# Another listed order for the first 1881 instructions of a fused attention and max-of-three-matmuls kernel

## The chip, the cores and the metric

The kernel runs on one core of one Trainium2 chip. Its time is the device time of one execution in microseconds (us); less is better. The core has five engines that work side by side, each with its own instruction stream that it takes strictly in order: PE (matmuls), DVE (vector work), ACT (activation functions and copies), POOL (elementwise work) and SP, which here only issues DMA transfers. An instruction that waits for another engine holds up everything listed behind it on its own engine.

## The reference

Local and global tokens attend to each other in 8 batches of 8 heads (512 local and 32 global tokens, head size 64). Local tokens see the global ones and a window of 32 to each side; global tokens see all. The heads are then joined and go through an elementwise maximum of three matmuls and a last matmul, all in f32:

```python
s_g = scale * np.matmul(q_g, k_all.transpose(0, 1, 3, 2))
out_g = np.matmul(sm(s_g), v_all)
s_ll = np.where(mask, scale * np.matmul(q_l, k_l.transpose(0, 1, 3, 2)), -1000000000.0)
s_l = np.concatenate([scale * np.matmul(q_l, k_g.transpose(0, 1, 3, 2)), s_ll], axis=-1)
out_l = np.matmul(sm(s_l), np.concatenate([v_g, v_l], axis=2))
x = np.concatenate([out_g, out_l], axis=2).transpose(0, 2, 1, 3).reshape(B * S, H * D)   # 4352 x 512 at S = 544
h = np.maximum(np.maximum(x @ w1, x @ w2), x @ w3)      # 512 -> 768, three times
out = h @ w_out                                          # 768 -> 512
```

## The kernel before

**Attention** goes slot by slot: a slot is 128 local tokens of a pair of heads. For each slot PE computes scores (`S`, or `pm` where they sit in a bank of the later matmuls; L368 from `kn` and `qn`, L372 from `kst` and `qs`); DVE evicts them with mask and row minimum (L375); ACT takes the exponential (L377); DVE sums and inverts (`z`, L379, L380); POOL or ACT scales (L120 to L124; in the first 16 slots the scaled tile is `s`, later `prob`, copied there by a DMA `prob<-s`); PE transposes (L408, `T`); ACT or DVE copies the transposed tile out (`pt`, L109 and L111; from slot 16 on in two steps, a rounded copy on ACT and the remainder by L103 on DVE); PE multiplies with V (L467 or L474, `O`); and `O` is evicted to `xr`. The 32 global tokens of each pair of heads take their own chain: scores at L294 or L298, their minimum at L302 and L310, the exponential on ACT at L311, the sum and its inverse on DVE at L312 and L313 (`zg`), the scaling to `probg`, and a transpose at L433, whose result goes into a bank of `S` and from there into `pt`.

**The matmuls behind it** work in rounded f32 with a remainder: every operand is held as a rounded half and what is missing (`xs` hi and lo, made from `xr` on ACT or DVE and on POOL at L103; weights `wh`/`wl`, `woh`/`wol`). L527 multiplies `xs` with `wh` and `wl` for the three weight matrices, twice hi and once lo; DVE takes the maximum (L535); the result is split into `h` (ACT L111, POOL L103); L546 multiplies with `woh`/`wol`.

**The weights** come in 24 pieces, `m` = 0 to 17 for `wh0` to `wh5` (three each) and six for `woh`. Each piece passes five engines in turn in `convert`: a DMA into `wraw`, ACT L162, POOL L165, DVE L169, L170 and L171 (through one PSUM bank `W` that all pieces share), ACT L174 (the rounded half), POOL L177 (the remainder).

**Order.** The body first issues the instructions in a nominal order; a running list of them is `traced`. Then `in_order` ties each instruction named in the table `FIRST` to the one named before it by a dependency without a semaphore, so that the table's order becomes the order of every engine's own stream; what the table does not name comes behind, in nominal order. `8+2` in the table means 8, 9, 10. Semaphores for data are as before in any order. The table covers the start, all weight pieces, the attention of slots 0 to 33 (two of the eight batches, and the start of the third) and the first matmuls behind it. Of a run of 821.5 us the listed part fills the first 172; behind it each engine's stream has the same order in both kernels.

The table is read at build time only:

```python
turn = [k for a, n in pairs for k in range(int(a), int(a) + int(n) + 1)]
for a, b in zip(turn, turn[1:]):
    tc.add_manual_dep(traced[b], traced[a].name, info, reason="order")
```

Of the kernel before, what the change touches and what calls it, by code (L numbers as in the profile page):

```python
# [687 lines left out]
8 4 0 5+1 9+2 1+1 13 7 3 45 14 138 15 217 26 304 37 39 52 54 40 16 38 17 65 27 41 76 28 42 12 113 18 53 20 19  # L688
29 99 21 31 1233 43 30 44 1281 22+1 46 24 32 47 77+1 25 50 33+1 48 79 35 80 49 55+1 51 36 66 81 67 57 82 59 58
105 167 68 60 84 70 85+2 69 61+1 106 71 63 83 107 64 88 72 89 73 90 108 74 119 134 120 75 135 91 93 100+1 92  # L690
251 102 136 103 121 94 109 157 123 114 137 104 115 95 110 116 96 117 139 122 141 158 97 118 129+1 142 131 98
132 159 124 198 140 152 161 143 111 133 144 153 148 154+1 125 199 145 126 150 160 156 127 173 346 162 128 146
193 200 194 151 195+1 163 168 201 169 164 174 170+1 183 175 202 177 172 165 176 197 213 166 178 203 236+1 208+2
112 211 204+1 238+1 184 206 179 147 212 234 190 180 214 235 181 240 207 182 280+3 187 149 186 188 408 226 409
189 228 185 227 410+2 229 413 264 432 438 230 215 192 265 216 439 218 440+1 220 442 219 452 221 453 222+2 241
272 242 225 191 252+2 243 255 257 245 231 244 454 259 246 266 477+2 256 1084 284 267 232 331 268 332+2 269 258
233 273 247 261 274 313 262 270 260 295+2 248 275 298 285+1 277 300 263 299 276 329 249 301 425 414 287 445 250
480 271 289 330 315 288 290 302 316 426+1 278 446+1 481+1 291 303 314 317+1 307 292 305 308 323 279 306 310+1
336+1 309 324 322 321 312 325 335 347+2 1282 350 338 320 352 356 363 340 293 364+2 319 294 368+1 355 339 494
370 351 353 372 569 341 378+1 326 380 327 381 342+1 383 385 415 357 416 367 354 358 371 403+2 382 406 360 359  # L700
384 373 433+2 344 417 361 436 328 443 387 345 386 390 388 401 393 407 374 428 448 389 483 418 472+1 375 474 419
362 475 394 868 395 484+1 420 402 396 437 444 376 568 429 476 486 430 449 377 450 397 495 487 496 456 504+1 391
421 506 392 422 507 488 515 545 431 546+1 455 457 548 558 451 398 500 497 489 501 423 502 458 503 510 508 511
424 516 512 399 513 459 514 517 464 518+1 543 521 460 522+1 498 524+2 490 549+1 400 509 551 461 552+1 491 465
554+1 557 544 466 559 570 462 571 467 499 572+3 560 576+1 469 520 578 468 579 561 581+1 492 583 556 584 580 463
585 493 528 589 529 591+1 527 593+1 590 595 562 596+2 530 599 470 617+3 1283 586 622 563 623+1 1098 531 626+1
621 628 535 629+1 564 631 587 471 565 641 536 642+1 640 632 644 532 566 645+1 634 852 647+1 533 588 649 537 650
653 633 654 656 538 601 600 657+1 625 659 661 635 662 539 663+2 651 666+1 660 655 567 668 689 534 669 691 636
692 652 540 602 693+1 696 637 697 670 698 541 690 699 603 700+3 695 704 609 604 705+2 639 709+1 605 671 711+2
715 606 542 610 717+2 638 720 714 611 721+1 724 672 725+1 723 612 727+2 673 731 708 732 716 733 751+2 613 754  # L710
756+2 755 759+1 763 730 761 608 762 607 764+1 776 674 614 777 781 775 766 782+1 681 784 768 767 785 675 786+2
615 791 676 793+1 769 734 795+1 678 797 677 798 789 800 824 801+1 804 683 805 799 616 825 806 682 807+2 684 826
679 827+1 735 829 831+1 778 833 830 834 685 835+1 838 779 840+1 770 686 680 736 790 853 771 792 780 854+1 737
851 856+2 743 803 859 738 860+2 876 837 877+1 687 879 739 880 884 772 886+1 863 888 842 773 885 889 688 890 744
891 844 892 740 774 893 864 894 843 912 881 913 810 914 916 745 845 917+3 741 921 746 933 839 865 747 934+1 931
748 936+2 846 882 742 847 939 866 940 867 941 811 848 812 942 945 883 946 849 948 813 895 949+1 953 749 954 817
850 955 922 956+2 915 814 907+1 923 909+1 959+1 924 961 750 818 975 815 947 976+1 911 962 978 869 819 991 925
992+1 896 870 820 943 994 968 1022 871 1023 821 816 1024+1 872 969 963 926 1002 944 1038 897 927 1039 873 822
1040+1 1003 874 964 898 970+3 875 1004 899 902 1049 974 1050+1 900 1068+3 928 903 1085 1007 1054 929 951 823
979 965 980 930 952 1008 932 981 995+2 983 998 901 990 982 1000 984 1009+1 904 1005 999 1055+1 905 1006 1057  # L720
1086 906 1042 1017+2 1001 1020 966 1043+2 985 1087 986 1021 1026 967 1011 1016 987 1012 1027 988 1046+1 989
1058 1028 1013 1030 1059 1029 1037 1060 1048 1052 1094 1014 1072+1 1031 1015 1088 1095 1106 1032 1107 1033 1083
1108 1074 1111 1113 1034 1076 1114 1053 1115 1061 1116 1096 1035 1097 1089 1112 1075 1063 1099 1064 1036 1065+1
1090+1 1077 1092 1062 1109 1117 1067 1118 1078 1125 1110 1100 1126+1 1093 1079 1128+2 1101 1080 1141 1081 1102
1142 1144 1131 1145+1 1133 1147 1103 1132 1148 1143 1120+2 1134 1104 1123 1149 1152 1124 1153 1135 1154 1105
1136 1157+1 1150 1159 1137 1160+1 1151 1082 1162+1 1138 1172+1 1155 1164 1174 1140 1175+1 1156 1177 1285 1165
1119 1188 1166 1139 1189+1 1284 1191+2 1187 1194 1178 1195 1287 1197 1180 1179 1199+1 1181 1201 1167+1 1198
1169+1 1196 1202 1204 1286 1206 1171 1207 1203 1208 1205 1209+2 1218 1182 1219 1183 1220+3 1184 1288 1234 1185
1213+1 1186 1215 1224 1216 1235 1237 1226 1238 1225 1390 1239+1 1236 1241 1217 1242 1391 1244 1227 1246+1 1212
1248 1245 1249 1243 1251+1 1228 1343 1253 1250 1298 1254+1 1229 1299 1256+1 1230 1266+2 1258 1269 1231 1270+1  # L730
1300 1259 1301 1232 1261 1302 1262+2 1272 1445 1289+1 1260 1303 1291 1274 1292 1265 1293+1 1304 1295 1273 1446
1296 1309+1 1275 1311 1305 1312 1314 1316 1297 1317 1313 1318 1306 1319 1276 1320 1315 1321 1323+1 1277 1325
1307 1326 1328+1 1278 1330 1327 1331+1 1308 1279 1333 1344 1392 1345 1347 1280 1334 1503 1348+1 1336 1350 1335
1351 1504 1352 1346 1355 1337 1356+1 1322 1358 1360 1353 1361 1338 1362 1359 1447 1363+1 1339 1354 1365+1 1340
1375+2 1367 1378 1341 1379+1 1509 1342 1393 1368 1370 1511 1371+1 1381 1373 1508 1394+1 1383 1396+2 1374 1399+1
# [93 lines left out]
```

## Time and profile before

| What | us |
| --- | --- |
| median of 3 runs | 824.18 |
| lowest, highest | 823.25, 825.42 |
| the profiled execution's own time | 823.32 |
| its span (first to last instruction) | 821.5 |
| left around the span | 1.8 |

The profile shows one execution. Engine names are PE, PEld (the weight loads that run beside PE's matmuls), DVE, ACT, POOL; `L527` is line 527 of the kernel before. A row of the timeline gives the start, the duration, the engine, the line, the output and inputs, and in brackets for how long the engine had been idle before and which instruction ended that. A row of the windows gives, for a stretch of the span, each engine's busy time and instruction count, then PE's granted clock (1.00 is full), the share of DMA and the GB/s moved.

### The profile page before, as it was taken

What the parts mean: (1) busy time and instruction counts of PE and PEld (TensorE: products, weight loads), DVE (VectorE), ACT (ScalarE), POOL (GpSimd) and SP (SyncE); (2) the same over time, 40 slices, a digit from 0 to 9 for tenths busy, and PEclk for the clock granted to TensorE, in tenths of its full rate; (3) what the DMA queues carried; (4) which work ended last, traced back from release to release, by engine and by line L of the source; (5) the groups of instructions that cost most, each with busy time, mean ns of one, the idle gap of its engine ahead of it and who ended that gap; (6) DMA issues with size and microseconds to landing.
All of it is one profiled execution on the core that took longest, in us unless ns stands there. A gap on an engine that the chain in (4) does not pass through costs nothing.

```text
span 821.5 us, 15804 instructions
## 1 busy us (share of the span) xinstructions
PE 799.7 (97%) x4548; PEld 677.1 (82%) x4548; DVE 528.4 (64%) x1819; ACT 520.4 (63%) x1496; POOL 513.0 (62%) x725
## 2 busy tenths in 40 slices
PE   6789999999999999999999999999999999999997
PEld 4469889978888888888888888888888888888886
DVE  5688855967676776767776766767776776411153
ACT  6698766867776777776776677676777666411210
POOL 4699846876676667857676676866776664311211
PEclk9899999999999999999999999999999999999999
DMA  8476643443345333343335333443335422100000
GB/s 280 136 249 212 211 144 119 142 129 104 107 116 154 104 111 102 108 141 105 105 107 168 104 105 110 126 136 91 102 95 173 111 82 63 61 14 0 26 26 26
DMA packets 106469, 94.55 MB, mean 115 GB/s; under 512 B 31504, under 2 KB 94864, under 8 KB 106384
## 3 DMA queue, kind: packets, MB, share of 16 engines
q1 hardware_dynamic: 106288, 93.43, 37.5%
q8 instruction: 36, 0.59, 0.3%
q14 instruction: 49, 0.40, 0.2%
q10 hardware_dynamic: 96, 0.13, 0.1%
HBM read 56.85 MB, written 8.91 MB: 80 GB/s over the span
## 4 chain that ended last, share of the span: by engine, by line
PE 92%; DVE 3%; ACT 2%; DMA 1%; POOL 1%; issue 1%; SPq 0%; DVEq 0%; ACTq 0%; POOLq 0%
PE pm L527 49%; PE pm L546 16%; PE O L474 7%; PE S L372 5%; PE T L408 4%; PE pm L512 2%; PE O L467 2%; PE S L298 2%; PE S L368 2%; PE pm L514 1%; PE S L433 1%; PE pm L368 1%; PE S L294 1%; DMA prob<-s 1%; ACT s L377 1%
## 5 line engine op out<-in xcount | busy, mean ns | idle before, releaser
L527 PE MATMUL pm<-xs,wh 128*128 128x512 f32 (+1 forms) x1296 | 394.9, 377 | 2.6 <-POOL xs L103 0.9
L527 PEld LDWEIGHTS pm<-xs,wh 128*128 128x128 f32 x1296 | 231.7, 190 | 35.1 <-issue 2.1
L527 PE MATMUL pm<-xs,wl 128*128 128x512 f32 (+1 forms) x648 | 242.2, 374 | 1.4 <-POOL wl L177 1.4
L124 POOL TENSOR_SCALAR s<-s,z 128x224 f32<-128x224 f32 (+1 forms) x244 | 104.1, 438 | 59.3 <-ACT lox L111 39.5
L527 PEld LDWEIGHTS pm<-xs,wl 128*128 128x128 f32 x648 | 122.9, 190 | 19.7 <-issue 2.0
L546 PE MATMUL pm<-woh,h 128*128 128x512 f32 x408 | 133.5, 398 | 0.0
L377 ACT ACTIVATE s<-s,nm 128x224 f32<-128x224 f32 (+1 forms) x256 | 118.2, 463 | 24.0 <-DVE nm L375 21.9
L103 POOL TENSOR_TENSOR h<-m,h 128x512 fp32r<-128x512 f32 (+1 forms) x60 | 68.7, 1145 | 96.1 <-ACT h L111 79.0
L103 DVE TENSOR_TENSOR pt<-T,pt 128x512 fp32r<-128x512 f32 (+2 forms) x126 | 69.7, 553 | 62.4 <-ACT pt L111 62.2
L103 POOL TENSOR_TENSOR qs<-qraw,qs 128x256 fp32r<-128x256 f32 x100 | 73.1, 739 | 48.7 <-ACT qs L111 42.4
L535 DVE TENSOR_TENSOR m<-pm,m 128x512 f32<-128x512 f32 (+1 forms) x108 | 67.5, 625 | 45.0 <-PE pm L527 44.1
L375 DVE CUSTOM_DVE_ANT_0 s<-S,mask 128x224 f32<-128x224 f32 (+1 forms) x240 | 79.9, 369 | 22.1 <-PE S L368 13.2
L546 PEld LDWEIGHTS pm<-woh,h 128*128 128x128 f32 x408 | 74.7, 188 | 13.5 <-issue 0.8
L111 ACT CAST pt<-T 128x512 fp32r<-128x512 f32 (+2 forms) x117 | 56.0, 479 | 39.2 <-PE S L433 24.5
L546 PE MATMUL pm<-wol,h 128*128 128x512 f32 x204 | 80.5, 395 | 0.0
L103 POOL TENSOR_TENSOR kst<-kraw,kst 64x576 fp32r<-64x576 f32 x50 | 71.3, 1425 | 13.7 <-issue 5.3
L103 POOL TENSOR_TENSOR vs<-vraw,vs 128x256 fp32r<-128x256 f32 x102 | 75.4, 740 | 7.0 <-ACT vs L111 5.5
L474 PEld LDWEIGHTS O<-pt,vs 128*128 128x128 f32 x408 | 66.5, 189 | 9.2 <-issue 0.6
L474 PE MATMUL O<-pt,vs 128*128 128x320 f32 (+1 forms) x408 | 73.3, 301 | 0.1
L111 ACT CAST qs<-qraw 128x256 fp32r<-128x256 f32 x99 | 40.2, 408 | 43.5 <-PE S L372 42.0
L372 PEld LDWEIGHTS S<-kst,qs 128*128 128x128 f32 x400 | 59.9, 191 | 8.7 <-issue 0.2
L482 DVE TENSOR_TENSOR xr<-O,lox 64x160 f32<-64x160 f32 x204 | 64.4, 316 | 3.5
(109 smaller groups left out, 1288.4 us busy)
## 6 DMA issues: line engine op xcount, KB each, us to landing
vraw<-v_in SPq DMA_DIRECT2D x64, 256.0 KB, 3.0
qraw<-q_in SPq DMA_DIRECT2D x100, 128.0 KB, 2.1
prob<-s SPq DMA_DIRECT2D x56, 224.0 KB, 2.4
wraw<-w_in SPq DMA_DIRECT2D x24, 512.0 KB, 4.1
out_dram<-o SPq DMA_DIRECT2D x32, 256.0 KB, 2.2
kraw<-k_in SPq DMA_DIRECT2D x25, 320.0 KB, 3.3
prob<-s SPq DMA_DIRECT2D x48, 128.0 KB, 2.2
prob<-s SPq DMA_DIRECT2D x48, 64.0 KB, 2.0
```

The source lines that it names most:

```text
L103: (dve if least(c) == "d" else pool).tensor_tensor(out=out, in0=a, in1=b, op=ALU.subtract)
L111: act.copy(out=out, in_=a)
L124: pool.tensor_scalar(out=out, in0=a, scalar1=col, scalar2=1.0, op0=ALU.mult, op1=ALU.mult)
L372: pe.matmul(ph[j][:, 0:n], lhsT=qs[i][:, a, 128 * j:128 * j + 128], rhs=kst[p][:, j, c0:c0 + n], start=(a == 0), stop=(a == 1))
L375: dve.tensor_tensor_reduce(out=s[:, j, 0:n], in0=ph[j][:, 0:n], in1=mask[:, (1, 0, 1, 0)[t], 32 * (t == 0):32 * (t == 0) + n], scale=-0.12 ...
L377: act.activation(out=s[:, j, 0:n], in_=s[:, j, 0:n], func=AF.Exp, bias=nm[:, j:j + 1], scale=-1.0, accum_out=ze[:, j, 0:1])
L408: pe.transpose(pr[0:w, 128 * x:128 * x + 128], s[:, 128 * x:128 * x + w], one)
L474: pe.matmul(o[:, j, 0:320].rearrange("p (a q) -> p a q", a=2)[:, :, 0:n], lhsT=vs[sl][:, 2 * j + c].rearrange("p a d -> p (a d)"), rhs=pt[ ...
L482: dve.tensor_tensor(out=xr[p][64 * j:64 * j + 64, t], in0=o[0:64, j, 0:160], in1=lo[:, j], op=ALU.add)
L527: pe.matmul(ps[:, 0:n], lhsT=w[f][:, i, k], rhs=xs[k][:, a, c0:c0 + n], start=(q == 0), stop=(q == 11))
L535: dve.tensor_tensor(out=m[:, 0:n], in0=ps[:, 0:n], in1=m[:, 0:n], op=ALU.max)
L546: pe.matmul(ps, lhsT=hh[f][:, a, 128 * t:128 * t + 128], rhs=w[:, f], start=(q == 0), stop=(q == 17))
```

## The change

The table `FIRST` is replaced by another. The old one lists 1881 instructions, the new one 1879 (the numbers 1848 and 1873, near the end, are left to the nominal order). Nothing else differs: the same instructions run, with the same operands, buffers and waits for data. The first lines of the two tables, with the rest left out:

```diff
@@ -685,74 +685,77 @@
 FIRST = """
-8 4 0 5+1 9+2 1+1 13 7 3 45 14 138 15 217 26 304 37 39 52 54 40 16 38 17 65 27 41 76 28 42 12 113 18 53 20 19
...
+5 45 10 4 304 8 0 11 6 9 14 13 7 217 15 138 16 52 1+1 17 3 54 27 12 28 26 18 37 20 19 53 29 39 21 31 38 65 30
+40 99 32 22 41 23 76 42 24 33+1 77 55 25 1233 43 35 44 56 49 36 51 66 57 48 46 78 59 79 58 80 47 82 67 113 50
...
 """
```

Since the new table is three lines longer, `in_order` and all behind it stand three lines lower; the lines of the body are the same.

What that does to the engines is seen in their streams. The first place is DVE in the first 30 us of the run, where the first three weight pieces (`W_361` with `wct_265`, `W_371` with `wct_311`, `W_423` with `wct_366`) and the soft-max sum of the second pair of global heads (`zg_349`) pass it. Before:

```order
L380 RECIPROCAL z_389<-z_389 128x2
L169 TENSOR_SCALAR W_361<-wct_265 128x512
L170 SCALAR_TENSOR_TENSOR W_361<-wraw_178,W_361 128x512
L171 SCALAR_TENSOR_TENSOR wct_265<-wraw_178,W_361 128x512
L169 TENSOR_SCALAR W_371<-wct_311 128x512
L170 SCALAR_TENSOR_TENSOR W_371<-wraw_210,W_371 128x512
L171 SCALAR_TENSOR_TENSOR wct_311<-wraw_210,W_371 128x512
L169 TENSOR_SCALAR W_423<-wct_366 128x512
L170 SCALAR_TENSOR_TENSOR W_423<-wraw_267,W_423 128x512
L171 SCALAR_TENSOR_TENSOR wct_366<-wraw_267,W_423 128x512
L312 TENSOR_SCALAR zg_349<-zg_349 64x1
L313 RECIPROCAL zg_349<-zg_349 64x1
```

And now, at the same place in DVE's stream:

```order
L171 SCALAR_TENSOR_TENSOR wct_265<-wraw_178,W_361 128x512
L379 TENSOR_REDUCE z_389<-z8_92 128x2
L169 TENSOR_SCALAR W_371<-wct_311 128x512
L380 RECIPROCAL z_389<-z_389 128x2
L312 TENSOR_SCALAR zg_349<-zg_349 64x1
L170 SCALAR_TENSOR_TENSOR W_371<-wraw_210,W_371 128x512
L313 RECIPROCAL zg_349<-zg_349 64x1
L171 SCALAR_TENSOR_TENSOR wct_311<-wraw_210,W_371 128x512
L169 TENSOR_SCALAR W_423<-wct_366 128x512
L170 SCALAR_TENSOR_TENSOR W_423<-wraw_267,W_423 128x512
L375 ISA s4_94,nm_443<-S_442,mask_89 128x224
```

The nine operations of the three pieces stood in one row ahead of `zg_349`; now `zg_349` passes behind four of them, the others are spread between steps of the attention, and the eviction of the next slot's scores (`S_442`) follows among them.

The second place is PE at that time. `pm_674`, `pm_703` and `pm_726` are the first outputs of L527, `S_418` the transpose of the second global pair, `S_442` the scores of slot 8, `T_435` and `T_500` transposes of slots 5 and 6 and `O_400`, `O_457` the products with V of slots 3 and 4. Before:

```order
L408 MATMUL T_500<-ident_82,s4_94 128x128 x4
L527 MATMUL pm_674<-xs_315,wh0_98 128x256 x2
L527 MATMUL pm_674<-xs_315,wl0_104 128x256
L527 MATMUL pm_674<-xs_432,wh0_98 128x256 x2
L527 MATMUL pm_674<-xs_432,wl0_104 128x256
L527 MATMUL pm_703<-xs_315,wh0_98 128x256 x2
L527 MATMUL pm_703<-xs_315,wl0_104 128x256
L527 MATMUL pm_703<-xs_432,wh0_98 128x256 x2
L527 MATMUL pm_703<-xs_432,wl0_104 128x256
L527 MATMUL pm_726<-xs_315,wh0_98 128x256 x2
L433 MATMUL S_418<-ident_82,probg_410 128x128
L368 MATMUL S_442<-kn_113,qn_242 128x224 x2
```

Now:

```order
L408 MATMUL T_380<-ident_82,s4_94 128x128 x4
L467 MATMUL O_400<-pt_323,vraw_180 64x160 x4
L527 MATMUL pm_674<-xs_315,wh0_98 128x256 x2
L408 MATMUL T_435<-ident_82,s4_94 128x128 x4
L433 MATMUL S_418<-ident_82,probg_410 128x128
L368 MATMUL S_442<-kn_113,qn_242 128x224 x2
L408 MATMUL T_500<-ident_82,s4_94 128x128
L294 MATMUL S_467<-kn_114,qg_115 64x384
L467 MATMUL O_457<-pt_385,vraw_263 64x160
L408 MATMUL T_500<-ident_82,s4_94 128x128
L294 MATMUL S_470<-kn_114,qg_115 64x160
```

Two of L527's fourteen matmuls are left ahead of `S_442`, none of them with a `wl`, and the rest comes behind.

The third place is the end of the listed part on PE. `O_2469` is a product with V of slot 32, `T_2432` the transpose of slot 33, `S_2485` and `S_2512` transposes of a global pair, `pm_2348` and `pm_2439` outputs of L546, and `pm_2518` the first output that is not in the table. Before:

```order
L474 MATMUL O_2469<-pt_2345,vs_2334 128x320 x4
L546 MATMUL pm_2439<-wol_111,h1_1746 128x512
L546 MATMUL pm_2439<-woh_110,h1_1746 128x512 x2
L546 MATMUL pm_2439<-wol_111,h1_1746 128x512
L546 MATMUL pm_2439<-woh_110,h2_2022 128x512 x2
L546 MATMUL pm_2439<-wol_111,h2_2022 128x512
L546 MATMUL pm_2439<-woh_110,h2_2022 128x512 x2
L546 MATMUL pm_2439<-wol_111,h2_2022 128x512
L433 MATMUL S_2485<-identr_87,probg_2401 128x128
L408 MATMUL T_2432<-identr_87,prob_1215 128x128 x4
L433 MATMUL S_2512<-identr_87,probg_2401 128x128
L527 MATMUL pm_2518<-xs_2259,wh0_98 128x512 x2
```

Now (nine more of L546's matmuls into `pm_2439` stand between the last row and the first of `pm_2518`):

```order
L474 MATMUL O_2469<-pt_2345,vs_2334 128x320 x4
L546 MATMUL pm_2348<-woh_110,h1_1746 128x512 x2
L408 MATMUL T_2432<-identr_87,prob_1215 128x128 x4
L433 MATMUL S_2512<-identr_87,probg_2401 128x128
L546 MATMUL pm_2348<-wol_111,h1_1746 128x512
L546 MATMUL pm_2348<-woh_110,h2_2022 128x512 x2
L546 MATMUL pm_2348<-wol_111,h2_2022 128x512
L546 MATMUL pm_2348<-woh_110,h2_2022 128x512 x2
L546 MATMUL pm_2348<-wol_111,h2_2022 128x512
L546 MATMUL pm_2439<-woh_110,h1_1746 128x512 x2
L546 MATMUL pm_2439<-wol_111,h1_1746 128x512
```

Two instead of ten of L546's matmuls stand between `O_2469` and the transposes of slot 33, and 19 instead of none between these and `pm_2518`. Over the whole listed part PE changes from one source line to another 325 times instead of 243.

On SP the first transfer is now that of `qn_118`, before that of `kn_113`, where the old order had `kn` and `qg` first; PE's first matmul is a score of slot 0 (L368, from `kn` and `qn`) instead of a global score (L294, from `kn` and `qg`).

136 rows, old and new, of the table FIRST are left out of this document.

## The prediction

> **What bounds the kernel now.** I read the page first, its sums and its 40 slices.
>
> ```profile
> span 821.5 us, 15804 instructions
> ...
> PE 799.7 (97%) x4548; PEld 677.1 (82%) x4548; DVE 528.4 (64%) x1819; ACT 520.4 (63%) x1496; POOL 513.0 (62%) x725
> ...
> PE   6789999999999999999999999999999999999997
> ...
> PEclk9899999999999999999999999999999999999999
> ```
>
> PE is busy for 799.7 of 821.5 us, and both kernels hold the same matmuls. So an order can win at most what PE stands idle, 21.8 us, and what it runs at a reduced clock. The slices put both into the first tenth of the span. The windows, cut where the listed part ends, say how much (columns: stretch, length, then busy us and instructions of PE, PEld, DVE, ACT and POOL, then PE's clock, DMA share, GB/s):
>
> ```profile
> 0.00:58.00 58.00, 42.43 (x245) 29.68 (x246) 40.46 (x151) 41.96 (x126) 37.92 (x70) 0.94 0.68 221
> 58.00:169.80 111.80, 111.65 (x833) 98.49 (x831) 82.02 (x279) 83.39 (x247) 86.92 (x124) 1.00 0.53 168
> 169.80:177.00 7.20, 5.33 (x25) 4.62 (x24) 3.82 (x14) 3.15 (x9) 4.20 (x6) 0.76 0.49 152
> 177.00:701.00 524.00, 523.94 (x2897) 447.15 (x2896) 367.64 (x1298) 370.46 (x1069) 363.60 (x506) 1.00 0.38 113
> 29.94:36.77 6.83, 5.57 (x21) 4.44 (x23) 3.42 (x10) 2.86 (x7) 4.80 (x7) 0.50 0.62 220
> 173.30:176.71 3.41, 3.41 (x13) 2.99 (x12) 1.44 (x7) 1.56 (x5) 1.44 (x2) 0.50 0.37 119
> ```
>
> 58.00 − 42.43 = 15.6 us of idle lie before 58 us, 0.15 between there and 169.8, 1.87 in the 7.2 us after, 0.06 to 701; the tail's rest is not in the listed part. In two stretches the clock is 0.50: matmuls that took 5.57 us would take half, 2.8 us lost; in the second 1.7 us. What the new order can touch is thus 15.6 + 0.15 + 1.87 + 4.5 = 22 us. Between 58 and 169.8 us it can only lose.
>
> What PE waits for in the head, from its timeline:
>
> ```profile
> 4.32 2.04 PE L294 MATMUL S<-kn,qg 128*64 128x384 f32 x4 [4.32 <-DMA qg<-k_in]
> 11.27 0.63 PE L408 MATMUL T<-ident,s 128*128 128x128 f32 x4 [1.83 <-DVE z L379]
> 27.81 0.63 PE L408 MATMUL T<-ident,s 128*128 128x128 f32 x4 [2.15 <-POOL xs L103]
> 29.31 0.51 PE L527 MATMUL pm<-xs,wh 128*128 128x256 f32 x2 [0.87 <-ACT wh L174]
> 30.67 0.58 PE L527 MATMUL pm<-xs,wl 128*128 128x256 f32 x1 [0.85 <-POOL wl L177]
> 34.71 1.70 PE L368 MATMUL S<-kn,qn 128*128 128x224 f32 x4
> 45.70 0.30 PE L433 MATMUL S<-ident,probg 128*128 128x128 f32 x1 [1.19 <-POOL probg L124]
> 56.03 0.39 PE L527 MATMUL pm<-xs,wh 128*128 128x256 f32 x1
> ```
>
> Six of these rows are waits, 4.32 to 0.85 us, and a DMA, DVE, POOL and ACT each end one or more: a chain through all engines, none of which is full. The common place shows on DVE and ACT:
>
> ```profile
> 26.46 0.69 DVE L169 TENSOR_SCALAR W<-wct 128x512 int32<-128x512 int32 x1 [1.35 <-POOL wct L165]
> 32.35 0.69 DVE L171 SCALAR_TENSOR_TENSOR wct<-wraw,W 128x512 int32<-128x512 int32 x1
> 32.95 0.14 DVE L312 TENSOR_SCALAR zg<-zg 64x1 f32<-64x1 f32 x1
> 28.64 0.62 ACT L174 CAST wh<-wct 128x512 fp32r<-128x512 f32 x1 [0.97 <-DVE wct L171]
> 30.82 0.62 ACT L174 CAST wh<-wct 128x512 fp32r<-128x512 f32 x1 [1.56 <-DVE wct L171]
> 33.07 0.62 ACT L174 CAST wh<-wct 128x512 fp32r<-128x512 f32 x1 [1.63 <-DVE wct L171]
> 33.71 0.85 ACT L122 ACTIVATE probg<-sg,zg 64x96 f32<-64x96 f32 x3
> 59.00 0.28 ACT L111 COPY xr<-O 128x160 f32<-128x160 f32 x1
> ```
>
> From 26.46 to 33.0 DVE does nothing but the three weight pieces. ACT stands for 0.97 + 1.56 + 1.63 = 4.2 us behind them, zg follows at 32.95, its scaling on ACT at 33.71, and only then PE can transpose it and go on to slot 8's scores, which start at 34.71. Everything that needs scores was without input for that time.
>
> **The change, part by part.** All sums are against the profiled execution's 823.3 us (821.5 of span and 1.8 around it); the median of the runs is 824.2, 0.9 more. No instruction is added or removed, so each term is idle time or clock.
>
> *Head, to slot 10's products: −7.5 (bounds −12.5 and 0).* I add up, per engine, the measured durations of what the order puts ahead of an instruction. `zg_349` has 17.2 us of DVE work ahead instead of 20.6, slot 8's scores 19.7 us of PE work instead of 23.6. The sizing point is `O_883`, slot 10's product with V: in the new order 40.4 us of PE work stand ahead of it, and the old PE had done that much at its row 56.03. It needs a copy of `xr` on ACT that has 36.5 us of ACT work ahead (87 instructions; 98 with 43.1 us before, where the copy is the row at 59.00). So it starts at 36.5 us plus what ACT idles until then. Before, ACT idled 58.00 − 41.96 = 16.0 us by 58. Of that the 4.2 us behind L171 go; what stays is ACT's start, about 7 to 8 us, and waits of a microsecond or two for scores: I take 12 (bounds 7 and 19.5). Then O_883 starts at 48.5 instead of 56.0, −7.5, which holds the 2.8 us of slow clock, and a late start worth +0.6:
>
> ```profile
> 0.73 1.28 ACT L311 ACT_TABLE_LOAD   x1 [0.73 <-PEq L820]
> 8.45 0.45 ACT L377 ACTIVATE s<-s,nm 128x192 f32<-128x192 f32 x1 [0.18 <-DVE nm L375]
> ```
>
> The table load, 1.28 us, ran at 0.73 with nothing to wait for. Now the first ACT instruction is slot 0's exponential, and the load carries its wait for the eviction; so that exponential comes near 9.1 instead of 8.45, and the first transpose near 11.9 instead of 11.27.
>
> The Trainium skill ("TensorE: Matmul & The Clock Gate", "Part 1: The HAM clock gate") says that the clock is decided over free-running windows of 4096 cycles, about 3.4 us, whose place against the kernel varies. The two slow stretches, 6.83 and 3.41 us long, agree. By that rule the 2.8 us are kept only if no window of the new head is as sparse, and a run may lose 1.7 us more or less than the next; the head's term would then lie between −4.7 and −7.5.
>
> *From 58 to about 110: +2.0 (bounds 0 and +6).* PE takes its attention earlier here (slot 14's product stands behind 57.5 us of PE work instead of 68.8), so all other engines must have done theirs earlier, and POOL is nearly full:
>
> ```profile
> 60.00:85.00 25.00, 25.00 (x208) 22.87 (x207) 22.29 (x59) 20.67 (x54) 23.49 (x31) 1.00 0.65 213
> 83.92 1.29 POOL L177 TENSOR_TENSOR wl<-wct,wh 128x512 fp32r<-128x512 f32 x1
> 90.52 0.28 PE L527 MATMUL pm<-xs,wl 128*128 128x256 f32 x1
> ```
>
> POOL works 23.49 of 25 us. The remainders of the weights have about 4 us more POOL work ahead than before (the last of `wl5` 66.2 instead of 62.2), and PE will be there some 7 us earlier. The slack was 90.52 − 85.21 = 5.3 us. 4 + 7 − 5.3 = 5.7 would be lost if nothing else gave; but POOL idled 58.00 − 37.92 = 20 us in the head too, and must idle less there if scores come earlier: I take a third.
>
> *Switching between kinds of matmuls: +1.0 (bounds 0 and +3.6).*
>
> ```profile
> 65.31 0.60 PE L408 MATMUL T<-ident,s 128*128 128x128 f32 x4
> 65.66 0.48 PE L527 MATMUL pm<-xs,wh 128*128 128x256 f32 x2
> 65.98 0.28 PE L527 MATMUL pm<-xs,wl 128*128 128x256 f32 x1
> ```
>
> 82 more changes of line are 41 round trips. Four transposes take 0.35 us from their start to the next kind, 0.09 each, and two matmuls of 256 columns 0.32. The rows overlap, and no change between them shows a gap. If each round trip cost a whole transpose it would be 41 × 0.09 = 3.6 us; by the rows it is nearer to nothing, and I take 1.0.
>
> *End of the listed part: −1.9 −1.7 +1.0 = −2.6 (bounds −3.6 and +0.5).*
>
> ```profile
> 160.32 0.46 PE L408 MATMUL T<-identr,prob 128*128 128x128 f32 x4
> 160.87 0.59 ACT L111 CAST pt<-T 128x512 fp32r<-128x512 f32 x1 [0.57 <-PE T L408]
> 161.49 0.69 DVE L103 TENSOR_TENSOR pt<-T,pt 128x512 fp32r<-128x512 f32 x1 [0.15 <-ACT pt L111]
> 169.42 0.39 PE L546 MATMUL pm<-wol,h 128*128 128x512 f32 x1
> 171.38 0.51 PE L408 MATMUL T<-identr,prob 128*128 128x128 f32 x4 [1.52 <-DMA prob<-s]
> 172.24 0.25 PE L433 MATMUL S<-identr,probg 128*128 128x128 f32 x1 [0.35 <-DMA probg<-sg]
> ```
>
> PE waits 1.52 and 0.35 us for slot 33's scaled scores, with the slow clock right behind. Those scores have PE work of about 11.1 us between them and the transposes now, 8.9 before; after the transposes 19 instead of no matmuls of L546 follow, 19 × 0.23 = 4.4 us (0.23 from one start to the next). The waits should go, 1.9, and the slow clock that followed them, 1.7. Against that, slots 21, 22, 26, 30 and 31 have only 1.2 to 2.4 us of PE work between their transposes and the product that needs them (3.1 to 6.1 before). From the transposes' end to the remainder's the rows above take 162.18 − 160.78 = 1.4 us. Some of the five will wait a few tenths: +1.0 for all.
>
> Sum: −7.5 + 2.0 + 1.0 − 2.6 = −7.1, so 816.2 for such an execution, and with the 0.9 a median of **817.0**.
>
> **The rivals.**
>
> *The vector engines eat the head start.* POOL is the bound from 50 to 110 us: the +2.0 becomes the whole 5.7. For it speaks its 94%; against it that it had 20 us of idle time before. 823.3 − 7.1 + 3.7 + 0.9 = 820.8.
>
> *Too little distance late.* In the five slots above ACT and DVE each finish one further operation first, 0.59 and 0.69 us: 1.4 + 1.3 = 2.7 us against 1.8 of work in the mean; 5 × 0.9 = 4.5 instead of the 1.0, so 820.5. For it speaks that PE has no slack to give there; against it that engines are two thirds busy and have work at hand.
>
> *Slower: the head blocks in order.* PE now takes attention steps one by one, between which L527 stood as filler. If each waits in turn for ACT, and ACT for DVE's evictions, then ACT idles more than before. The mechanism sits at O_883, each microsecond of ACT's idle time above 12 costs one. At 19.5 the head's gain is nothing, and the sum with the other terms is 823.3 + 0.4 + 0.9 = 824.6; from about 21.6 it is measurably slower; at 24 it would be 829. For it speaks that 12 of L527's 14 matmuls went from ahead of slot 8's scores to behind; against it, that they were themselves waited for (0.87 and 0.85 us), and that DVE is no longer blocked.
>
> That the new table leaves the engines' order as it was is no rival: the three places shown above differ.
>
> **How the numbers follow.** A measurement of this kernel tells about 0.3% (2.5 us) from no change: faster is below 821.7, slower above 826.7. The forecast, with the head's gain between 5 and 10: 0.60 (0.52 faster, 0.08 the same where a term strays). POOL as bound 0.17 and late slots 0.10: both near 820.6, so 0.22 faster and 0.05 the same. Both together, 824: 0.03 (0.02 the same, 0.01 slower). Blocked head 0.10, slower. That gives faster 0.74, same 0.15, slower 0.11. The range: low end 811.5, where the head wins 3 us more, the part behind it loses 2 less and the end wins 0.5 more; high end 823.5, which takes in both middle rivals and leaves out the blocked head, the two together and a few in a hundred of the rest.
>
> **What would show it.** Right: PE's idle time before 58 us falls from 15.6 to about 8, the DVE stretch of nine L169 to L171 is gone, slot 8's scores start near 29, the remainder of `xs` that PE needs for slot 10 is ready near 46; no wait for `prob<-s` at the listed part's end, and clock 1.00 behind it. The listed part's last transpose, with the 19 matmuls behind it counted in, ends 7 us earlier. Wrong: PE idle of more than 3 us between 58 and 170, with POOL L177 or DVE pt as releaser; or ACT idle of 16 us or more before 50. Clock 0.50 anywhere in the head or behind 165 us would take the clock's part back.

## The result and the profile after

The new order takes **815.96 us** (median of 4 runs, 814.04 to 816.29) against 823.78 for the old one (823.25 to 825.42): a ratio of 0.9897, with a 95% interval of 0.9876 to 0.9918. The forecast was 817.0, with a range of 811.5 to 823.5. The profiled execution took 815.84, its span 814.0.

The page of the new kernel, its sums and two of its slice rows:

```profile
span 814.0 us, 15780 instructions
...
PE 798.2 (98%) x4548; PEld 674.2 (83%) x4548; DVE 523.4 (64%) x1819; ACT 518.8 (64%) x1496; POOL 513.6 (63%) x725
...
PE   6899999999999999999999999999999999999997
...
PEclk9999999999999999999999999999999999999999
```

The span is 7.5 us shorter, yet PE's busy time fell by only 1.5 (799.7 to 798.2). PE's idle time fell by 6.0: 821.5 − 799.7 = 21.8 before, 814.0 − 798.2 = 15.8 now. The windows say where (busy us and instructions of PE, PEld, DVE, ACT, POOL, then clock, DMA share, GB/s):

```profile
0.00:50.00 50.00, 40.61 (x258) 28.95 (x259) 33.36 (x145) 40.27 (x129) 34.98 (x70) 1.00 0.74 242
50.00:58.00 8.00, 8.00 (x58) 6.57 (x58) 7.54 (x24) 6.97 (x21) 7.04 (x11) 1.00 0.42 134
58.00:110.00 52.00, 50.60 (x356) 41.78 (x357) 44.04 (x133) 39.86 (x111) 44.58 (x56) 1.00 0.69 222
110.00:162.30 52.30, 51.55 (x397) 46.65 (x394) 32.60 (x131) 36.35 (x115) 39.16 (x59) 1.00 0.44 136
162.30:170.00 7.70, 7.70 (x39) 6.54 (x39) 3.63 (x13) 3.93 (x11) 3.27 (x4) 1.00 0.40 137
```

Before 58 us PE idles 9.4 us (15.6 before); between 58 and 162.3 us it idles 2.15 (0.15 before); at the end of the listed part not at all (1.87 before). No window above shows a clock under 1.00. In the eight runs of the new order (these four and those of e0 below) the mean granted clock was 0.997 to 1.000, in the 53 runs of the old order beside the experiments 0.987 to 0.996.

The windows print 1.00 also where the profile has no clock record, and it has none before 9.46 us in the old run and before 7.70 us in the new one. PE ran at half speed there. In the old run eight matmuls of L368 took twice as long before the first record as behind it:

```profile
6.29 3.14 PE L368 MATMUL pm<-kn,qn 128*128 128x192 f32 x8
11.73 1.57 PE L368 MATMUL pm<-kn,qn 128*128 128x192 f32 x8
```

The first eight in the new run took 3.11 us. Before the first record PE was busy for 5.12 us in the old run and for 3.13 us in the new one, and half of that was lost to the clock too.

For the old and all other kernels below I split PE's time up to the first matmul behind the listed part (`pm_2518`) into three: idle (no PE row covers it), clock (half of its busy time in stretches at clock 0.50 and before the first clock record), and what is left, busy time at full clock. The matmuls are the same in all, so that the third would be equal if order were free. It is good to 1 or 2 us where much of the run is slow: e6 below differs from the old order on PE in 30 places only and has 1.6 us less.

| Kernel | listed part ends | idle | lost to the clock | busy at full clock |
| --- | --- | --- | --- | --- |
| old order | 172.33 | 17.60 | 5.35 | 149.38 |
| new order | 166.49 | 11.53 | 1.56 | 153.40 |

−6.1 idle, −3.8 clock, +4.0 busy: −5.8 before rounding; behind the listed part another 1.7 of slow clock is gone. That is the 7.5.

### The profile page after: what moved, and what is told of

Read it like the earlier page. It is cut to its first block, busy times and chain, and to the rows that moved or that the text cites. A ratio compares the mean times of both kernels' runs of the same rounds, so it can differ in the third digit from the quotient of the medians.

```text
span 814.0 us, 15780 instructions
## 1 busy us (share of the span) xinstructions
PE 798.2 (98%) x4548; PEld 674.2 (83%) x4548; DVE 523.4 (64%) x1819; ACT 518.8 (64%) x1496; POOL 513.6 (63%) x725
## 4 chain that ended last, share of the span: by engine, by line
PE 93%; ACT 3%; DMA 2%; DVE 1%; issue 1%; SPq 0%; POOL 0%; ACTq 0%; DVEq 0%
PE pm L527 49%; PE pm L546 17%; PE O L474 7%; PE S L372 5%; PE T L408 4%; PE pm L512 2%; PE O L467 2%; PE S L298 2%; PE S L368 1%; DMA prob<-s 1%; PE S L433 1%; PE pm L514 1%; ACT s L377 1%; DMA wraw<-w_in 1%; PE S L294 1%; PE pm L368 1%
## 5 line engine op out<-in xcount | busy, mean ns | idle before, releaser
L527 PE MATMUL pm<-xs,wh 128*128 128x512 f32 (+1 forms) x1296 | 391.9, 376 | 0.8 <-ACT wh L174 0.8
L527 PEld LDWEIGHTS pm<-xs,wh 128*128 128x128 f32 x1296 | 230.5, 189 | 32.9 <-issue 1.6
L527 PE MATMUL pm<-xs,wl 128*128 128x512 f32 (+1 forms) x648 | 241.1, 373 | 0.0
L527 PEld LDWEIGHTS pm<-xs,wl 128*128 128x128 f32 x648 | 122.1, 189 | 16.3 <-issue 0.3
L546 PE MATMUL pm<-woh,h 128*128 128x512 f32 x408 | 133.9, 399 | 0.0
L377 ACT ACTIVATE s<-s,nm 128x192 f32<-128x192 f32 (+1 forms) x256 | 118.2, 463 | 14.1 <-DVE nm L375 12.3
L546 PEld LDWEIGHTS pm<-woh,h 128*128 128x128 f32 x408 | 74.5, 188 | 12.6 <-POOL h L103 0.3
L546 PE MATMUL pm<-wol,h 128*128 128x512 f32 x204 | 81.0, 397 | 0.0
L372 PEld LDWEIGHTS S<-kst,qs 128*128 128x128 f32 x400 | 60.4, 189 | 9.0 <-issue 0.5
```

Source lines behind the costliest of these rows:

```text
L372: pe.matmul(ph[j][:, 0:n], lhsT=qs[i][:, a, 128 * j:128 * j + 128], rhs=kst[p][:, j, c0:c0 + n], start=(a == 0), stop=(a == 1))
L377: act.activation(out=s[:, j, 0:n], in_=s[:, j, 0:n], func=AF.Exp, bias=nm[:, j:j + 1], scale=-1.0, accum_out=ze[:, j, 0:1])
L527: pe.matmul(ps[:, 0:n], lhsT=w[f][:, i, k], rhs=xs[k][:, a, c0:c0 + n], start=(q == 0), stop=(q == 11))
L546: pe.matmul(ps, lhsT=hh[f][:, a, 128 * t:128 * t + 128], rhs=w[:, f], start=(q == 0), stop=(q == 17))
```

## The head in the new trace

PE's timeline of the new kernel at the places of the prediction (in brackets how long PE had been idle, and what ended it):

```profile
4.57 3.11 PE L368 MATMUL pm<-kn,qn 128*128 128x192 f32 x8 [4.57 <-DMA kn<-k_in]
10.11 0.30 PE L408 MATMUL T<-ident,s 128*128 128x128 f32 x1 [1.34 <-DVE s L120]
25.49 0.50 PE L527 MATMUL pm<-xs,wh 128*128 128x256 f32 x2 [0.81 <-ACT wh L174]
26.76 0.92 PE L368 MATMUL S<-kn,qn 128*128 128x224 f32 x4
34.88 0.77 PE L467 MATMUL O<-pt,vraw 128*64 128x160 f32 x8 [0.92 <-ACT xr L111]
46.27 0.71 PE L467 MATMUL O<-pt,vraw 128*64 128x160 f32 x8
49.93 0.63 PE L408 MATMUL T<-ident,s 128*128 128x128 f32 x4 [0.67 <-ACT pt L111]
89.52 0.28 PE L433 MATMUL S<-identr,probg 128*128 128x128 f32 x1 [1.11 <-ACT pt L111]
```

Slot 8's scores start at 26.76 (34.71 before), `O_883` at 46.27. Up to there PE was busy for 37.55 us and ACT for 37.27 (columns as above):

```profile
0.00:46.27 46.27, 37.55 (x233) 26.39 (x233) 32.92 (x144) 37.27 (x121) 31.37 (x64) 1.00 0.75 241
```

No wait for `wl` is left. DVE in the new kernel, where the nine operations stood:

```profile
24.31 0.69 DVE L169 TENSOR_SCALAR W<-wct 128x512 int32<-128x512 int32 x1
24.92 0.15 DVE L380 RECIPROCAL z<-z 128x2 f32<-128x2 f32 x1
24.99 0.12 DVE L312 TENSOR_SCALAR zg<-zg 64x1 f32<-64x1 f32 x1
25.04 0.69 DVE L170 SCALAR_TENSOR_TENSOR W<-wraw,W 128x512 int32<-128x512 int32 x1
```

`zg` passes at 24.99 instead of 32.95. And ACT's start:

```profile
6.72 1.28 ACT L377 ACT_TABLE_LOAD   x1 [6.72 <-DVE nm L375]
8.02 0.46 ACT L377 ACTIVATE s<-s,nm 128x192 f32<-128x192 f32 x1
```

The table load did move behind the first eviction, as forecast. But the scores now come first on PE, at 4.57 instead of 6.29, so that the exponential starts at 8.02, 0.4 earlier than before and not 0.6 later.

The last of the PE rows above, at 89.52, waits for a copy on ACT. That copy (89.27) stands behind a weight piece which itself waited for its transfer:

```profile
88.70 0.66 ACT L162 ACTIVATE wct<-wraw 128x512 f32<-128x512 f32 x1 [1.71 <-DMA wraw<-w_in]
```

## The experiments

All are other tables of the same kernel; `old` and `new` are the two lists. The times of the old kernel beside them had medians of 822.9 to 823.4. Its runs spread over 821.3 to 828.0, so I read the experiments by PE's three parts.

**e1, only the head**

```diff
-turn = old
+turn = new[:457] + [k for k in old if k not in new[:457]]
```

> The new table's first 457 entries (up to slot 10's product O_883, which the new trace starts at 46.3 us), then everything else in the old table's sequence. Theory A (the gain is made in the head, and what is lost behind it is PE's own slower pace between more changes of line): PE reaches the same amount of work 9 to 10 us earlier than before, behind it the old order costs nothing, so about 814 to 815 with the old waits at the end of the listed part (1.9 us and a slow clock of 1.7) still there. Rival B (the other engines, POOL above all, cannot follow an early PE, whatever PE's order): PE waits 4 us or more between 50 and 120 us, and the time is 818 or more.

820.4 us (ratio 0.9965, 0.9952 to 0.9978). The head runs as in the new kernel, then PE stands at the seam (timeline and window of e1):

```profile
56.02 0.79 PE L527 MATMUL pm<-xs,wh 128*128 128x256 f32 x2 [6.25 <-ACT m L111]
```

```profile
54.00:60.83 6.83, 4.81 (x22) 4.81 (x23) 6.20 (x10) 5.03 (x10) 5.78 (x8) 0.50 0.56 190
```

6.25 us of waiting, for a copy of `m` on ACT that the old order has behind weight work, and a slow stretch around it (half of 4.81 is 2.4 us). Behind it no wait above 0.12 us until the old waits at the end, 1.97 us. By its marks (a wait of 4 us or more, 818 or more) this is rival B, but the theories are not told apart: the cut itself makes a wait that neither table has. What e1 does show is that old order behind the head gives a busy time of 149.09 us at full clock, 0.3 less than the old kernel's and 4.3 less than the new one's. The 4.0 us more of busy time thus lie behind the head.

**e2, the end from entry 1800 on**

```diff
-turn = old
+turn = old[:1800] + [k for k in new if k not in old[:1800]]
```

> The old table's first 1800 entries (to about 164 us), then the rest in the new table's sequence: ten matmuls of L546 move from ahead of slot 33's transposes to behind them. Prediction's term: the waits of 1.52 and 0.35 us and the slow clock behind them go, 3.6 us, so about 820.2. Rival: the transposes, now ten matmuls (2.3 us) earlier in PE's stream, wait that much longer for the same DMA, so that nothing is gained: 823.8.

828.3 us (1.0053, 1.0035 to 1.0070): slower. PE's timeline at the end:

```profile
172.09 0.26 PE L433 MATMUL S<-identr,probg 128*128 128x128 f32 x1 [2.94 <-DVE xr L482]
...
175.16 0.51 PE L408 MATMUL T<-identr,prob 128*128 128x128 f32 x4 [1.12 <-DMA prob<-s]
176.02 0.25 PE L433 MATMUL S<-identr,probg 128*128 128x128 f32 x1 [0.35 <-DMA probg<-sg]
```

4.4 us of waits instead of 1.87: by the waits, the rival. The transposes come earlier in PE's stream, what they wait for doesn't. The cut moves more than PE's ten matmuls, though: DVE's stream differs from the old one in 18 places and ACT's in 6, and the longest wait is by its row one for DVE, which the rival did not name. By the profile the end is a draw: 1.9 us more idle time, and no slow stretch behind the listed part, where the old order loses 1.7. The rest of the difference is slow clock in the head, whose order is unchanged (11.4 us lost instead of 5.4; the first clock record comes only at 17.17 us). Why it was so slow there is not shown.

**e3, head and end**

```diff
-turn = old
+turn = new[:457] + (old[:1800] without those) + (the rest of new)
```

> Head as in the new table (457 entries), then the old table's sequence up to its entry 1800, then the new one's end. Theory A: the head's 9.8 us and the end's 3.6 us add up, without the new table's middle: 823.8 - 9.8 - 3.6 = 810.4, with waits of 1 to 2 us somewhere in the middle 811 to 812.5. Rival B: the middle eats the head start whatever the order, 816 or more.

824.1 us (1.0014, 0.9994 to 1.0034): e1's seam again (6.17 us), waits like e2's (3.4 us behind 160 us), and 7.9 us lost to slow clock. The pieces of an order don't add up.

**e10 and e11, the end with all engines.** At entry 1300 the two tables have the same instructions behind them but for 16, so the cut is nearly clean.

```diff
-turn = old
+turn = old[:1300] + [k for k in new if k not in old[:1300]]   # e10
+turn = new[:1300] + [k for k in old if k not in new[:1300]]   # e11
```

> The old table's first 1300 entries (to 128 us of the old run), then the rest in the new table's sequence on all engines. At this cut the two tables have put the same instructions behind them but for 16. Theory E (the end's waits go where the scores of slot 33 stand further ahead on all engines, not PE's matmuls alone, as e2 showed): no wait for prob or probg at the end of the listed part, no half clock behind it: PE idle of the listed part 1.9 us less than before. Rival (the end was won because the head start left room on every engine): 1 us or more of waits for prob or probg remain, as in e2.

> The complement of e10: the new table's first 1300 entries, then the old table's sequence. Theory E: the waits for prob and probg at the listed part's end are back, 1.9 us, in spite of the head start, and perhaps 1.7 us of half clock: 817.5 to 819.5. Rival (the head start leaves room): no such wait, 815 to 816.

e10: 823.6 us (1.0013, 0.9991 to 1.0034); no wait at the end of the listed part (0.13 us in all behind 160 us) and no slow clock behind it, but 2.1 us of waits, most of them around the cut, and 1.3 us more busy time, which give it back. e11: 816.4 us (0.9931, 0.9916 to 0.9945), and at its end:

```profile
164.78 0.51 PE L408 MATMUL T<-identr,prob 128*128 128x128 f32 x4 [1.70 <-DMA prob<-s]
165.55 0.25 PE L433 MATMUL S<-identr,probg 128*128 128x128 f32 x1 [0.27 <-DMA probg<-sg]
```

The old end brings the old waits, 1.97 us, and the slow stretch of 3.41 us behind them (1.7 us lost), in spite of the head start. So the end's gain belongs to the order behind entry 1300; the head start gives it no room. What in that order does it can be read off PE's rows. From the end of slot 33's last scores (L372) to its transposes (L408) it is 6.02 us in the old kernel and in e2 and 6.03 in e11, each with a wait of 1.1 to 1.7 us in it. It is 7.87 us in the new kernel and 7.86 in e10, without a wait. In e10:

```profile
160.73 0.38 PE L372 MATMUL S<-kst,qs 128*128 128x224 f32 x2
...
168.97 0.46 PE L408 MATMUL T<-identr,prob 128*128 128x128 f32 x4
```

In these three runs the scores take 6 us to come back as `prob`; the two orders with more PE work than that in between have no wait. e11's time stays below its expected 817.5 to 819.5, since it also drops waits of the new order between 110 and 160 us (0.11 instead of 0.74 us) and before, and has 1.4 us less busy time (151.97 against 153.40).

**e6 and e7, the block on DVE.** e6 undoes the block in the old order, e7 puts it back into the new one. PE in e6 (before and after rows of its stream), and DVE in e7:

```diff
 L527 MATMUL pm<-xs,wh_98 128x256 x2
+L433 MATMUL S<-ident,probg 128x128
+L368 MATMUL S<-kn,qn 128x224 x2
+L467 MATMUL O<-pt,vraw 64x160 x2
...
 L527 MATMUL pm<-xs,wl_104 128x256
```

```diff
 L171 SCALAR_TENSOR_TENSOR wct<-wraw,W 128x512
+L169 TENSOR_SCALAR W<-wct 128x512
+L170 SCALAR_TENSOR_TENSOR W<-wraw,W 128x512
+L171 SCALAR_TENSOR_TENSOR wct<-wraw,W 128x512
...
 L379 TENSOR_REDUCE z<-z_92 128x2
...
 L312 TENSOR_SCALAR zg<-zg 64x1
```

> The old table with the one blockage of the head undone by hand: on DVE zg_349's two operations go ahead of weight pieces two and three, and piece three behind slot 8's evictions; the scaling of probg_410 goes ahead of weight work on ACT and POOL; on PE S_418, S_442, O_457 and the two global scores go ahead of the matmuls that need wl0. Theory A (that block is the cause of the head's loss): slot 8's scores start near 30 instead of 34.7 and PE idles 3 to 5 us less before 60 us; 819 to 820.5. Rival B (the gain is the new order of the whole head; one chain freed only meets the next wait): slot 8's scores come earlier, but PE idles less than 1 us less by 60 us; 823 or more.

> The new table with the nine operations of the first three weight pieces put back in one row on DVE, ahead of zg_349 and z_389; all other engines as in the new table. Theory A: zg_349 and what follows comes 3 to 3.5 us later (five operations of 0.69 us), and as the new order has no other work ahead on PE there, most of it stays: 818 to 819.5. Rival B (DVE's block does not bound): within 1 us of the new kernel, 815 to 817.

e6: 826.7 us (1.0028, 1.0003 to 1.0053). PE's timeline of e6:

```profile
30.12 1.70 PE L368 MATMUL S<-kn,qn 128*128 128x224 f32 x4
...
36.68 0.39 PE L527 MATMUL pm<-xs,wl 128*128 128x256 f32 x1 [0.85 <-POOL wl L177]
...
40.04 0.48 PE L433 MATMUL S<-ident,probg 128*128 128x128 f32 x1 [2.17 <-DVE nmg L302]
```

The scores do come 4.6 us earlier, and nothing is won: PE meets the next wait, 2.17 us at 40.04. Idle time in the listed part is 18.4 us (17.6 in the old order), and 8.3 us go to the clock (5.4). By the idle time that is the rival.

e7: 821.0 us (0.9966, 0.9949 to 0.9982), where the new kernel beside it took 815.5. PE in e7:

```profile
30.24 0.47 PE L433 MATMUL S<-ident,probg 128*128 128x128 f32 x1 [3.48 <-POOL probg L124]
```

One wait of 3.48 us, the five operations of 0.69, and with it a slow stretch of 6.83 us: idle 13.9 us and clock 3.7, against 10.2 and 1.6 in the new kernel's run beside it. 3.6 + 2.0 less 0.4 of busy time are the 5.3 us (before rounding) by which the listed part ends later. So in the new order the block would cost all that theory A said and more; in the old one, taking it away gives nothing. It bounds only when all that stands beside it is in step.

**e5, more changes of line**

```diff
-L408 MATMUL T<-ident,s_94 128x128 x4
-L527 MATMUL pm<-xs,wh_100 128x256 x2
+L408 MATMUL T<-ident,s_94 128x128
+L527 MATMUL pm<-xs,wh_100 128x256
+L408 MATMUL T<-ident,s_94 128x128
+L527 MATMUL pm<-xs,wh_100 128x256
+L408 MATMUL T<-ident,s_94 128x128
 L527 MATMUL pm<-xs,wl_106 128x256
+L408 MATMUL T<-ident,s_94 128x128
```

> The old order, with one thing changed on PE: in 20 groups of four transposes between 60 and 168 us, the next three matmuls of L527 or L546 are put between the four (T M T M T M T). PE changes line 355 times instead of 243 in the listed part. Theory A (each change of line costs PE about 0.036 us, from 3.1 us more busy time at 86 more changes between before and after): 112 x 0.036 = 4.0 us, so 827.8, with as much more busy time of PE and no more idle time. Rival C (changes are free, and PE's busy time rose for another cause): 823.8 within 0.7, and PE's busy time as before.

825.7 us (1.0019, 1.0000 to 1.0038). The head of this run lost more to the clock (8.6 us, its first clock record comes at 16.16 us), so I take PE's records 261 to 1047, which are the same matmuls in both: 105.06 us busy at full clock against 103.83 in the old kernel. 1.23 us for 112 changes, 0.011 us each. Neither theory: a change isn't free, but the 82 more of the new order explain 0.9 of its 4.0 us.

**e8, e9 and e12, products with V.** A matched comparison of every matmul of old and new put most of the rest on L467. Its matmuls use half of the array's columns (`128*64` in the rows), two for each half. The old order leaves three slots' products in pieces, the new one ten. The busy time of L467 alone (windows for that line: stretch, length, busy of PE and PEld with counts, clock, DMA, GB/s), in the old kernel, then the new one:

```profile
0.00:180.00 180.00, 20.80 (x208) 12.92 (x208) 0.97 0.57 184
```

```profile
0.00:180.00 180.00, 24.23 (x208) 14.37 (x208) 1.00 0.59 187
```

The same 208 records take 3.4 us more. e9 makes the ten whole in the new order, e12 only the seven behind 50 us, and e8 takes ten apart in the old order:

```diff
-L467 MATMUL O<-pt,vraw 64x160 x3
 L294 MATMUL S<-kn 64x160
-L467 MATMUL O<-pt,vraw 64x160
+L467 MATMUL O<-pt,vraw 64x160 x4
```

```diff
-L467 MATMUL O<-pt,vraw 64x160 x4
+L467 MATMUL O<-pt,vraw 64x160
 L527 MATMUL pm<-xs,wh_100 128x256
+L467 MATMUL O<-pt,vraw 64x160 x2
+L527 MATMUL pm<-xs,wl_106 128x256
+L467 MATMUL O<-pt,vraw 64x160
```

> The old table with ten products with V between 60 and 142 us taken apart on PE: the four matmuls O1 O2 O3 O4 become O1 M O2 O3 M O4, where M are the next two matmuls of L527. The inverse of e9. Theory D (neighbours of 128*64 run side by side, e9 has 0.36 us for each product made whole): 10 x 0.36 = 3.6 us more full-clock busy time of PE in the listed part, little more idle time. Rival C (a change costs 0.012 us): 40 more changes, 0.5 us.

> The new table with one change on PE: where the four matmuls of a slot's product with V (L467, halves of the array, 128*64) stand apart, the first three go behind to the fourth, 10 slots. Theory D (two matmuls of 128*64 that follow each other run side by side: x8 records take 0.69 us in a row, but x2 alone 0.42): 0.2 to 0.3 us for each of 10 slots, so 2 to 3 us less PE busy time and 813 to 814. Rival C (a change of line costs 0.012 us, as 1.3 us over 112 changes has it, whatever the kind): 14 changes fewer, 0.2 us, so as the new kernel, 816.

> As e9, but only the seven products with V that stand apart behind 50 us are made whole; the three in the head stay as in the new table. Theory D: 7 x 0.36 = 2.5 us less busy time than the new kernel, and without e9's wait of 2.26 us at 50.7 us nearly all of it is kept: 813 to 813.5. Rival F (PE is then held by the other engines, ACT's copies above all, so that the time won on PE comes back as idle time, as in e9): 814.5 to 815.5.

e8: 831.1 us (1.0103, 1.0082 to 1.0124). Its L467 takes 27.61 us:

```profile
0.00:180.00 180.00, 27.61 (x208) 13.90 (x208) 0.98 0.56 178
```

6.8 us more than in the old order, and PE's busy time at full clock in the listed part is 7.8 us more (157.2): twice what was expected, most likely since each of the ten was cut at two places and not one. PE's timeline of e8, one of these products:

```profile
68.35 0.48 PE L467 MATMUL O<-pt,vraw 128*64 128x160 f32 x2
68.77 0.39 PE L527 MATMUL pm<-xs,wh 128*128 128x256 f32 x1
69.08 0.49 PE L467 MATMUL O<-pt,vraw 128*64 128x160 f32 x4
69.51 0.38 PE L527 MATMUL pm<-xs,wl 128*128 128x256 f32 x1
```

One matmul (two records) takes 0.42 us from its start to the next, two neighbours 0.43. So two halves side by side cost what one costs alone. That need not be all of a cut's price. A whole product (`x8`, two such pairs) takes 0.64 us to the next start (46.27 to 46.91 in the new kernel), so its second pair adds only 0.21: a piece that starts anew has about 0.2 us of its own. A cut between the two pairs, which would show that part alone, was not run. The Trainium skill ("TensorEngine Tiling (Array Packing)", "Overview") promises up to twice the speed for matmuls that need 64 of the columns; the trace agrees, for neighbours in the stream.

e9: 814.4 us (0.9871, 0.9839 to 0.9903); L467 takes

```profile
0.00:180.00 180.00, 19.69 (x208) 12.71 (x208) 1.00 0.59 189
```

and PE's busy time at full clock in the listed part is 150.0 us instead of 153.4 and 153.6 in two profiles of the new kernel: 3.4 to 3.6 us less, more than the 2 to 3 expected, and all but 0.6 of its surplus over the old order. But idle time rose to 13.4 us (11.5 and 10.2 in those two profiles). The largest wait, with its cause on ACT:

```profile
50.70 0.63 PE L408 MATMUL T<-ident,s 128*128 128x128 f32 x4 [2.26 <-ACT pt L111]
```

```profile
49.42 0.66 ACT L162 ACTIVATE wct<-wraw 128x512 f32<-128x512 f32 x1 [2.34 <-DMA wraw<-w_in]
```

ACT stands in order behind a weight piece whose transfer has not landed. e12: 813.8 us (0.9895, 0.9873 to 0.9918); busy 150.6, idle 12.5, of which 0.6 us is a later first transfer (PE starts at 5.23 us, at 4.57 and 4.67 in the two profiles of the new kernel). Both expectations are half right in each: the busy time falls by what was said or more, and a part comes back as idle time. The medians are 1 to 2 us below the new kernel's, but the intervals overlap that of the new kernel run beside e9 (e0):

> The new kernel once more, beside the others on one chip: 815 to 817, PE idle about 9.4 us before 50 us, no half clock.

815.5 us (0.9889, 0.9856 to 0.9922), PE idle 9.4 us before 60 us, no half clock. Whether e9 or e12 is faster than the new order stays open; in both the time on PE is less.

The three parts of all these kernels, as above:

| Kernel | listed part ends | idle | lost to the clock | busy at full clock |
| --- | --- | --- | --- | --- |
| e0, new again | 165.48 | 10.24 | 1.63 | 153.61 |
| e1, new head | 170.76 | 16.71 | 4.96 | 149.09 |
| e2, new from 1800 on | 179.40 | 19.50 | 11.40 | 148.50 |
| e3, both | 176.11 | 18.73 | 7.92 | 149.46 |
| e5, more changes | 176.49 | 17.64 | 8.61 | 150.24 |
| e6, block undone in old | 174.50 | 18.43 | 8.33 | 147.74 |
| e7, block back in new | 170.74 | 13.85 | 3.65 | 153.24 |
| e8, products cut in old | 179.64 | 17.32 | 5.13 | 157.19 |
| e9, products whole in new | 164.91 | 13.39 | 1.54 | 149.98 |
| e10, new from 1300 on | 173.76 | 17.90 | 5.15 | 150.71 |
| e11, old from 1300 on | 165.63 | 11.18 | 2.48 | 151.97 |
| e12, seven products whole | 164.85 | 12.45 | 1.79 | 150.61 |

## Why the prediction was right, and where it was not

The sum was −7.1 against the profiled execution and the trace shows −7.5. That it came so close is in part luck: its terms missed in both directions. It also left out the half clock at the start, 2.56 us lost before and 1.56 now, since the windows print 1.00 there. Of its signs, PE's idle time before 58 us fell to 9.4 us and not to about 8, slot 8's scores came at 26.76 and not near 29, and the listed part ended 5.8 us earlier and not 7; no wait for `prob<-s` and no slow clock at the end came true.

- **Head, −7.5: measured −9.8** (`O_883` at 46.27, where the old order had done as much PE work, by the prediction's count, at 56.03). The path was right: ACT's copy of `xr` ran from 45.92 to 46.21, just ahead of `O_883`. ACT's 36.5 us of work ahead were counted right too (37.27 busy by 46.27, some of it behind the copy). PE had been busy for 37.55 us and not 40.4, a count that took durations of the old trace, half-clock ones among them. The 9.8 us hold 3.8 of clock, where 2.8 were forecast. The term that was sized wrong is ACT's idle time until then, taken as 12: it was 46.27 − 37.27 = 9.0 us. The start is not what differs, for in the first 10 us ACT idles 6.74 us now and 6.80 before. Behind 10 us it idles 2.26 up to `O_883`, where it idled 9.24 up to 58 us before: 7.0 less, and the prediction had taken off 4.2. The late start was forecast wrong as well, +0.6 taken and −1.2 measured at the first transpose (10.11, not 11.9): the table load did cost its 1.28 us, but I had left out that PE's scores of slot 0 no longer stand behind the 2 us of global scores.
- **The cause named for the head** (nine weight operations in a row on DVE): e7 shows that the new order can't bear it, 5.4 us. e6 shows that taking it out of the old order gives nothing: ACT's waits for L171 before 58 us rise from 4.7 to 6.7 us there. So the block must go, but that alone is not enough. The prediction took the work ahead from sums over whole engines, but the idle time that it took off, 4.2 us, from this one chain; which other moves free the rest of the 7.0 us no run here shows.
- **58 to 110 us, +2.0 for POOL and the weights:** PE idled 2.15 us between 58 and 162 us, so the size fits, but by luck: the reason does not. No PE wait there has `wl` behind it. The largest, 1.11 us at 89.52, waits for a copy on ACT behind a weight piece that itself waited for its transfer, as in e9. So the weights are in it, but by a transfer and not by POOL. Another profile of the new kernel (e0) has 0.86 us of idle time from 60 to 160 us, where this one has 2.14. The rival in which POOL eats the head start fell with it.
- **Switching, +1.0: measured +4.0** of busy time at full clock, above the bound of 3.6. The term itself was well sized: by e5, changes of line as such cost 0.011 us each, 0.9 for 82. What I did not see was that the products' halves are pushed apart, 3.4 us on L467 by its windows, which e9 takes back and e8 makes at will.
- **End, −2.6: measured −1.9 − 1.7 + 0.3.** Waits and slow clock both went. Of the two reasons given, L546's matmuls as cover behind the transposes is not it: with them moved behind and the old order up to entry 1800 (e2) the waits grow. The longer distance on PE between scores and transposes is (7.87 us instead of 6.02; e10, e11). The waits for the five short distances stayed at 0.12 and 0.14 us, which are part of the 2.15 above.
- **The blocked head** did not come: ACT idled 9.0 us, where the rival began at 19.5.

## What to carry to other kernels

Time an order by the work listed ahead on each engine, not by the one blockage that shows: a block taken out alone uncovers the next wait, and the same block put back into an order that is in step costs its full length and more. Splitting a run of matmuls of half the array's width costs PE time (3.4 to 3.6 us for ten products here), so they have to stay neighbours when a scheduler spreads work finely. A wait moves if only its consumer is moved: more work than its producers take (6 us at the end here) has to be listed between them. And look where the profile's clock records begin before calling a stretch full speed.

## What was not expected of the hardware

Two neighbouring matmuls of `128*64` took 0.43 us, one alone 0.42. Half-clock stretches were 3.41, 6.83 or 10.24 us long, and came after some waits and not after others: after 1.87 us of waits in the old kernel (1.7 us lost), after 1.97 in e11, but not after 1.97 in e1 or 4.4 in e2. PE ran at half speed from its first matmul up to 9.46 us in the old kernel's first profile, up to 16.16 in e5 and 17.17 in e2. With that, the same table's head lost 5.4 us in the first profile, 8.6 in e5 and 11.4 in e2. The Trainium skill ("TensorE: Matmul & The Clock Gate", "Part 1: The HAM clock gate") speaks of free-running windows of about 3.4 us; the lengths agree with it, and so does it that the same wait is followed by a slow stretch in one run and not in another. The five profiles with the new order's head and no added wait (the new kernel, e0, e9, e11 and e12) show none in the head behind the start.
